# Causal attention with a two-layer cosine block: ScalarE's copies placed ahead of an exponential, and a new order in steps 0 and 1

## The chip, the cores and the metric

One core of a Trainium2 chip runs one program. The time is the device time of one execution in microseconds (us), from three runs. The engines named below are TensorE (PE), VectorE (DVE), ScalarE (ACT), GpSimd (POOL) and SyncE (SP), which issues most DMAs.

## The reference

Inputs: q, k and v of shape 4 x 12 x 448 x 64 (batch, heads, sequence, head dimension), `w_in` 768 x 2048 and `w_out` 2048 x 768, all float32. Causal attention is computed per head, the heads are laid side by side into x of 1792 x 768, and a two-layer block with h cos(h) between its products follows:

```python
scores = scale * np.matmul(q, k.transpose(0, 1, 3, 2))
scores = np.where(mask, -1000000000.0, scores)      # mask: above the diagonal
scores = scores - np.max(scores, axis=-1, keepdims=True)
attn = np.exp(scores)
attn = attn / (np.sum(attn, axis=-1, keepdims=True) + 1e-09)
x = np.matmul(attn, v)                              # then heads side by side
h = x @ w_in
out = (h * np.cos(h)) @ w_out
```

## The kernel before

The kernel has two stages that follow each other: `attention` (to about 160 us) and `moe` (the rest). The instructions of each engine run in the order in which the source issues them; the order below is written out by hand.

**Attention** works on 24 pairs of heads (4 batches x 6 pairs), `N = 24`, one a step. The loop at line 479 has 28 turns, because a pair passes through four steps: in step i-2 its q and k are loaded (`load_qk`), in step i-1 they are transposed (`transpose_in`, line 307, four transposes each) and copied from PSUM to SBUF (`evac_in`, line 319), in step i its probabilities are made, in step i+1 these are normalised and transposed (`tp`, line 400), and in step i+2 they are multiplied with v (`av`, line 421) and the output is split into a high and a low part (`finish_hi`, `finish_lo`).

A pair's 448 rows are cut into blocks m = 1 to 7 of 64 rows and 64 m columns; the two heads lie in the two halves of the 128 partitions, so block 7 is 128 x 448 and block 1 is 128 x 64. For a block, in order: `scores` (line 354, TensorE into PSUM banks 4 to 7), `masked` (line 363, VectorE: mask added, maximum taken, result to SBUF), `exps` (line 371, ScalarE: exponential and row sum, followed by a short read of the sum), `inverse` (lines 378 and 379, VectorE, for several blocks at once), `normalise` (line 385, GpSimd, in place). `FIRST` is blocks 7, 4, 3, which are normalised in their own step; `SECOND` is blocks 6, 1, 5, 2, which are normalised in the next step, after its first masking.

`tp` transposes 128 x 128 pieces of the probabilities in four groups (numbers 0 to 3) into PSUM banks; `evac_tp` copies a group to SBUF at line 315 (VectorE, groups 0 and 3) or 317 (ScalarE, groups 2 and 1). Group 1 is last and reuses bank 3, which group 0 left.

`finish_hi` (line 456, ScalarE) copies the output of `av` from PSUM rounded to fp32r, and `finish_lo` (line 460, VectorE) subtracts this from the output; `finish_lo` needs `finish_hi`.

In steps from 2 on, the orders of the engines are these. ScalarE: exponentials of 7, 4, 3, 6; `finish_hi`; copy of q for the next step; exponential of 1; copy of k; exponential of 5; copy of group 2; exponential of 2; copy of group 1. VectorE: masking of 7; inverse of `SECOND`; masking of 4, 3, 6, 1, 5, 2; inverse of `FIRST`; `finish_lo`; copies of groups 0 and 3; then, after the step's `yield`, half of the conversion of a weight piece (`convert_weight`, line 131: lines 139 and 142 in even steps, 148 and 152 in odd ones). GpSimd: normalising of 6, 1, 5, 2; what the conversion left to it (`postponed`, lines 145 or 156 and 157); normalising of 7, 4, 3. TensorE: scores; `av`; transposes of q; group 0; transposes of k; groups 3, 2, 1.

Before the loop, q and k of step 0 are copied in two halves by VectorE and ScalarE, and `keep_warm` issues matmuls on zeros that nothing reads.

**moe** multiplies x with the weights, which the attention stage and its own earlier groups have loaded and split into two fp32r parts.

Of the kernel before, what the change touches and what calls it, by code (L numbers as in the profile page):

```python
# [21 lines left out]
def kernel(  # L22
# [205 lines left out]
    def attention(filler_of, postponed):  # L228
        with (
# [53 lines left out]
            def keep_warm(n):  # L283
                for _ in range(n):
                    nc.tensor.matmul(
                        banks8[:, 0, 0:P], lhsT=warm, rhs=warm, start=True, stop=True
                    )
# [19 lines left out]
            def transpose_in(i, which, b):  # L307
                t = qkt[i, which] = flat[:, 2 * which + i % 2, 0:S], banks8[:, b, 0:S]
                o = t[1].rearrange("p (r c) -> p c r" if which else "p (c r) -> p c r", c=4)
                for c in range(4):  # L310
                    nc.tensor.transpose(o[:, c], nat[i][which][:, c], ident[0:Q4, 0:Q4])  # L311
# [7 lines left out]
            def evac_in(i, which, dve=False, rs=slice(0, Q4)):  # L319
                d, s = qkt[i, which]  # L320
                d = d.rearrange("p (r c) -> p r c", c=4)
                s = s.rearrange("p (r c) -> p r c" if which else "p (c r) -> p r c", c=4)
                evac(d[:, rs], s[:, rs], dve)
# [36 lines left out]
            def masked(i, *ms):  # L360
                for m in ms:
                    z = W if m == TURNED else S - m * R
                    nc.vector.tensor_tensor_reduce(  # L363
                        out=probs(i, m), in0=place(m), in1=mask[:, z : z + m * R], scale=-scale,
                        scalar=3.0e38, op0=ALU.add, op1=ALU.min, accum_out=stats[i][:, 0, col(m)],
                    )

            def exps(i, *ms):
                for m in ms:
                    st = stats[i]  # L370
                    nc.scalar.activation(  # L371
                        probs(i, m), probs(i, m), AF.Exp, scale=-1.0, bias=st[:, 0, col(m)],
                        accum_out=st[:, 1, col(m)],
                    )
# [3 lines left out]
                nc.vector.tensor_scalar(st[:, 2, cs], st[:, 1, cs], 1e-9, None, op0=ALU.add)  # L378
                nc.vector.reciprocal(st[:, 2, cs], st[:, 2, cs])  # L379

            def normalise(i, *ms):
                for m in ms:
                    p = probs(i, m)
                    r = stats[i][:, 2, col(m)]
                    nc.gpsimd.tensor_tensor(p, p, r.to_broadcast(list(p.shape)), op=ALU.mult)  # L385

# [11 lines left out]
            def tp(i, n, b, o=0):  # L400
                for x, (m, kc) in enumerate(ORDER[n]):
                    a = AT[m] + (m - 1 if kc == NM else 2 * kc + (m == TURNED))
                    nc.tensor.transpose(  # L403
                        banks8[:, b, o + x * P : o + (x + 1) * P],
                        prob[i][:, a * R : (a + 2) * R], ident,
                    )
# [14 lines left out]
            def av(i):  # L421
                (vn, vo), o = vals.pop(i), o_of(i).rearrange("p (n r) -> p n r", r=R)
                pt = ptr[i].rearrange("p n (s r) -> p n s r", r=R)
                for a in range(2):
                    s = spots[LAST[a][0], NM]
                    for y, m in enumerate(LAST[a]):
                        ys = slice(y * R, (y + 1) * R)
                        for j in range(2):
                            nc.tensor.matmul(
                                o[heads(j), ROW.index(m)],  # L430
                                lhsT=(vo[ys, a, i % 2] if y else vn[ys, m // 2])[:, heads(j)],
                                rhs=pt[ys, s, j ^ SWAP[m]],
                                start=a == 0, stop=False,
                            )
                runs = [((2, 4), 0), ((3, 5), 0), ((6,), 0), ((7,), 0), ((4, 5), 1), ((6, 7), 1), ((6, 7), 2)]
                for x, (ms, kc) in enumerate(runs):
                    s, z, n = spots[ms[0], kc], ROW.index(ms[0]), len(ms)
                    step = ms[-1] - ms[0] or 1
                    for j in range(2):
                        nc.tensor.matmul(  # L440
                            o[heads(j), z : z + step + 1 : step] if n == 2 else o[heads(j), z : z + 1],
                            lhsT=vn[:, kc, heads(j)], rhs=pt[:, s : s + n, j ^ SWAP[ms[0]]],
                            start=False, stop=x in (4, 6),
                        )
# [9 lines left out]
            def finish_hi(i):  # L454
                for hi, _, cs in x_of(i):
                    nc.scalar.copy(hi, o_of(i)[:, cs])

            def finish_lo(i):
                for hi, lo, cs in x_of(i):
                    nc.vector.tensor_tensor(lo, o_of(i)[:, cs], f32(hi), op=ALU.subtract)  # L460
# [3 lines left out]
            def fill(n):  # L464
                if not extra:
                    spare = itertools.cycle((7, 6))
                    extra.append(filler_of(lambda: banks8[:, next(spare)]))
                for _ in zip(range(n), extra[0]):
                    pass

            transpose_in(0, 1, 7)
            evac_in(0, 1, True, slice(0, Q4 // 2))
            evac_in(0, 1, False, slice(Q4 // 2, Q4))
            keep_warm(14)
            transpose_in(0, 0, QB)
            evac_in(0, 0, True, slice(0, Q4 // 2))
            evac_in(0, 0, False, slice(Q4 // 2, Q4))
            keep_warm(10)
            for i in range(N + 4):
                cur, prev, nxt = i < N, 0 < i <= N, i + 1 < N  # L480
                old = 0 <= i - 2 < N
                if i + 2 < N:
                    load_qk(i + 2)
                if prev:
                    load_v(i - 1)
                if cur:
                    open_step(i)
                    scores(i)
                    masked(i, 7)
                if prev:  # L490
                    inverse(i - 1, SECOND)
                    normalise(i - 1, *SECOND)
                while postponed:
                    postponed.pop(0)()
                if cur:
                    exps(i, 7)
                    masked(i, 4, 3)
                    if i == 0:
                        exps(i, 4)
                        transpose_in(i + 1, 0, QB)  # L500
                        evac_in(i + 1, 0, True)
                        transpose_in(i + 1, 1, 3)
                        evac_in(i + 1, 1)
                        keep_warm(8)
                        exps(i, 3)
                    else:
                        exps(i, 4, 3)
                    masked(i, 6, 1)
                    exps(i, 6)
                    masked(i, 5, 2)  # L510
                    inverse(i, FIRST)
                    normalise(i, *FIRST)
                if i == N + 2:
                    run(extra[0])
                if old:
                    av(i - 2)
                    finish_hi(i - 2)
                    finish_lo(i - 2)
                if nxt and i:
                    transpose_in(i + 1, 0, QB)  # L520
                    evac_in(i + 1, 0)
                if i == 1:
                    transpose_in(i + 1, 1, 1)
                    evac_in(i + 1, 1)
                if prev:
                    open_ptr(i - 1)
                    tp(i - 1, 0, 3)
                    evac_tp(i - 1, 0, 3, True)
                if N - 2 < i < N + 2:
                    fill((4, 12, 11)[i + 1 - N])  # L530
                if cur:
                    exps(i, 1)
                if nxt and i > 1:
                    transpose_in(i + 1, 1, 6)
                    evac_in(i + 1, 1)
                if cur:
                    exps(i, 5)
                if prev:
                    tp(i - 1, 3, 5)
                    evac_tp(i - 1, 3, 5, True)  # L540
                    tp(i - 1, 2, QB)
                    evac_tp(i - 1, 2, QB)
                if cur:
                    exps(i, 2)
                if prev:
                    tp(i - 1, 1, 3)
                    evac_tp(i - 1, 1, 3)
                yield i

    def m1_sum(ring, g, fi, t0, n, hv):  # L550
# [64 lines left out]
    def run(*gens):  # L615
        for x in gens:
            for _ in x:
                pass
# [777 lines left out]
```

## Time and profile before

| what | us |
|---|---|
| median of 3 runs (lowest, highest) | 615.96 (615.55, 619.16) |
| the profiled execution: its time | 615.92 |
| the profiled execution: span, first to last instruction | 613.9 |
| PE busy, share of the span | 599.3 (98%) |
| DVE busy | 474.6 (77%) |
| POOL busy | 451.8 (74%) |
| ACT busy | 409.2 (67%) |

Busy time counts the instructions on an engine; matmuls are pipelined and their ends are modelled, so a busy PE is not a PE at its peak. The mean granted TensorE clock was 0.999 of full speed. A row of a timeline gives the start, the duration, the engine, the line, the operation, what it wrote and read, and, in brackets, how long the engine had been idle before it and whose work ended that. Instructions of one kind in a row are merged into one row (x3).

### The profile page before, as it was taken

What the parts mean: (1) busy time and instruction counts of PE and PEld (TensorE: products, weight loads), DVE (VectorE), ACT (ScalarE), POOL (GpSimd) and SP (SyncE); (2) the same over time, 40 slices, a digit from 0 to 9 for tenths busy, and PEclk for the clock granted to TensorE, in tenths of its full rate; (3) what the DMA queues carried; (4) which work ended last, traced back from release to release, by engine and by line L of the source; (5) the groups of instructions that cost most, each with busy time, mean ns of one, the idle gap of its engine ahead of it and who ended that gap; (6) DMA issues with size and microseconds to landing.
All of it is one profiled execution on the core that took longest, in us unless ns stands there. A gap on an engine that the chain in (4) does not pass through costs nothing.

```text
span 613.9 us, 13441 instructions
## 1 busy us (share of the span) xinstructions
PE 599.3 (98%) x4788; PEld 546.6 (89%) x4788; DVE 474.6 (77%) x1017; ACT 409.2 (67%) x928; POOL 451.8 (74%) x529
## 2 busy tenths in 40 slices
PE   8999999999999999999999999999999999999996
PEld 7777787787788999999999999999999999999996
DVE  5899999999557788877778877754377887887786
ACT  5988888898677778787778777732435644653540
POOL 2767777687528879787777787753579888878994
PEclk9999999999999999999999999999999999999999
DMA  7656657558307859797796969489997559549104
GB/s 160 156 122 172 164 132 180 137 129 230 78 17 258 316 195 339 273 302 276 250 322 203 325 222 334 171 317 394 402 362 279 176 165 308 205 149 316 54 0 155
DMA packets 127010, 134.18 MB, mean 219 GB/s; under 512 B 75072, under 2 KB 111280, under 8 KB 126944
## 3 DMA queue, kind: packets, MB, share of 16 engines
q1 hardware_dynamic: 119264, 106.92, 55.6%
q0 software_dynamic: 4928, 24.78, 11.0%
q10 hardware_dynamic: 2752, 1.64, 0.9%
q8 instruction: 38, 0.62, 0.4%
q14 instruction: 28, 0.23, 0.1%
HBM read 83.36 MB, written 49.94 MB: 217 GB/s over the span
## 4 chain that ended last, share of the span: by engine, by line
PE 89%; DVE 6%; ACT 2%; POOL 1%; issue 1%; DVEq 0%; POOLq 0%; ACTq 0%
PE banks L652 22%; PE banks L1081 12%; PE banks L1101 12%; PE banks L557 7%; PE banks L558 7%; PE banks L556 7%; PE banks L354 5%; PE banks L440 5%; PE banks L403 3%; DVE pm L315 2%; PE banks L311 2%; PE banks L1118 2%; PE banks L1005 2%; DVE xa L460 2%; ACT pb L371 1%; DVE xb L460 1%
## 5 line engine op out<-in xcount | busy, mean ns | idle before, releaser
L640 DVE TENSOR_TENSOR acc<-acc,banks 128x768 f32<-128x768 f32 (+1 forms) x122 | 112.6, 932 | 43.6 <-PE banks L652 33.4
L385 POOL TENSOR_TENSOR pb<-pb,stat 128x448 f32<-128x448 f32 (+6 forms) x168 | 98.6, 617 | 45.5 <-DVE stat L379 43.3
L652 PE MATMUL banks<-w,gh 128*128 128x384 f32 x512 | 109.8, 335 | 0.0
L371 ACT ACTIVATE pb<-pb,stat 128x448 f32<-128x448 f32 (+6 forms) x168 | 84.9, 506 | 20.4 <-DVE stat L363 11.8
L652 PEld LDWEIGHTS banks<-w,gh 128*128 128x128 f32 x512 | 90.8, 188 | 1.5 <-DVE acc L638 0.2
L557 PE MATMUL banks<-xa,w 128*128 128x512 f32 x192 | 75.2, 391 | 0.0
L558 PE MATMUL banks<-xa,w 128*128 128x512 f32 x192 | 75.0, 391 | 0.0
L556 PE MATMUL banks<-xa,w 128*128 128x512 f32 x192 | 74.8, 390 | 0.0
L652 PE MATMUL banks<-w,gl 128*128 128x384 f32 x256 | 65.1, 335 | 0.0
L363 DVE CUSTOM_DVE_ANT_0 pb<-banks,mask 128x448 f32<-128x448 f32 (+6 forms) x168 | 61.2, 418 | 2.7 <-PE banks L354 2.7
L676 POOL TENSOR_TENSOR w<-ct,w 128x768 fp32r<-128x768 f32 x28 | 51.9, 1852 | 14.4 <-ACT w L675 9.1
L403 PE MATMUL banks<-ident,pb 128*128 128x128 f32 x336 | 52.9, 280 | 7.0 <-DVE pm L315 4.2
L564 ACT ACTIVATE ni<-banks 128x512 int32<-128x512 f32 (+1 forms) x64 | 34.4, 538 | 32.7 <-PE banks L558 19.2
L583 POOL TENSOR_TENSOR gl<-r,gh 128x512 fp32r<-128x512 f32 x32 | 41.5, 1298 | 19.5 <-ACT gh L582 19.2
L403 PEld LDWEIGHTS banks<-ident,pb 128*128 128x128 f32 x336 | 36.6, 141 | 17.0 <-DVE pm L315 9.5
L566 DVE SCALAR_TENSOR_TENSOR r<-ni,banks 128x512 f32<-128x512 int32 (+1 forms) x56 | 35.0, 626 | 21.4 <-ACT ni L564 20.7
L568 ACT ACTIVATE r<-r 128x512 f32<-128x512 f32 (+1 forms) x56 | 32.8, 586 | 22.4 <-DVE r L566 21.9
L652 PEld LDWEIGHTS banks<-w,gl 128*128 128x128 f32 x256 | 46.4, 188 | 0.0
L571 DVE SCALAR_TENSOR_TENSOR r<-r,banks 128x512 f32<-128x512 f32 (+1 forms) x56 | 35.0, 626 | 13.6 <-ACT r L569 13.6
L1081 PE MATMUL banks<-xb,bb 128*128 128x384 f32 x234 | 44.7, 334 | 0.0
L558 PEld LDWEIGHTS banks<-xa,w 128*128 128x128 f32 x192 | 36.0, 188 | 7.5
L1101 PE MATMUL banks<-big,gh 128*128 128x384 f32 x168 | 42.6, 334 | 0.0
(138 smaller groups left out, 1484.9 us busy)
## 6 DMA issues: line engine op xcount, KB each, us to landing
bb<-w_in_d SPq DMA_DIRECT2D x48, 384.0 KB, 5.2
land<-in_moe_w_in_dram SPq DMA_DIRECT2D x14, 768.0 KB, 6.0
land<-in_moe_w_out_dram SPq DMA_DIRECT2D x14, 768.0 KB, 5.6
w_out_d<-w POOLq DMA_DIRECT2D x14, 768.0 KB, 5.5
big<-w_out_d SPq DMA_DIRECT2D x25, 384.0 KB, 4.4
w_in_d<-w POOLq DMA_DIRECT2D x7, 768.0 KB, 4.3
raw_d<-ct POOLq DMA_DIRECT2D x14, 384.0 KB, 7.5
land<-in_k_dram SPq DMA_DIRECT2D x46, 112.0 KB, 3.2
```

The costliest lines, as they stand in the source:

```text
L363: nc.vector.tensor_tensor_reduce(out=probs(i, m), in0=place(m), in1=mask[:, z : z + m * R], scale=-scale, scalar=3.0e38, op0=ALU.add, op1= ...
L371: nc.scalar.activation(probs(i, m), probs(i, m), AF.Exp, scale=-1.0, bias=st[:, 0, col(m)], accum_out=st[:, 1, col(m)],)
L385: nc.gpsimd.tensor_tensor(p, p, r.to_broadcast(list(p.shape)), op=ALU.mult)
L403: nc.tensor.transpose(banks8[:, b, o + x * P : o + (x + 1) * P], prob[i][:, a * R : (a + 2) * R], ident,)
L556: yield nc.tensor.matmul(hv, lhsT=wh[:, f], rhs=x[:, 0, cc, t], start=(cc == 0), stop=False)
L557: yield nc.tensor.matmul(hv, lhsT=wh[:, f], rhs=x[:, 1, cc, t], start=False, stop=False)
L558: yield nc.tensor.matmul(hv, lhsT=wl[:, f], rhs=x[:, 0, cc, t], start=False, stop=(cc == NCC - 1))
L640: nc.vector.tensor_tensor(d, d, o, op=ALU.subtract)
L652: nc.tensor.matmul(o[:, e, 0:EH], lhsT=a[:, cs], rhs=w[:, e * EH : (e + 1) * EH], start=(x == 0), stop=(x == 5),)
L676: nc.gpsimd.tensor_tensor(w[:, 1], tf, f32(w[:, 0]), op=ALU.subtract)
L1081: nc.tensor.matmul(o, lhsT=w[:, u, k * P : (k + 1) * P], rhs=x[k][:, v], start=k + m == 0, stop=k == K - 1 and m == 2,)
L1101: nc.tensor.matmul(o[:, b % 2, 0:EH], lhsT=g_ops[i][u][:, c * P : (c + 1) * P], rhs=wouts[g, i][:, v], start=(x == 0), stop=(x == 2),)
```

## The change

`normalise` can be given an engine. In steps 2 to 23, ScalarE does `finish_hi` and the copy of q before the exponential of block 6, and the copy of k before that of block 1; the orders of the other engines are as they were. For step 0, q and k are copied whole, k by ScalarE and q by VectorE, with 8 warming matmuls behind instead of 10. Steps 0 and 1 get branches of their own: in step 0 the exponential of 3 comes ahead of the copy of k, and the inverse and normalising of `FIRST` ahead of the masking of 5 and 2. In step 1 VectorE makes the copies of q and k and normalises blocks 1 and 2 of step 0, the inverse of `SECOND` comes after the masking of 4 and 3, GpSimd normalises 6 and 5 alone, and group 1 goes to bank 0, ahead of groups 3 and 2.

```diff
-            def normalise(i, *ms):
+            def normalise(i, *ms, eng=nc.gpsimd):
                 for m in ms:
                     p = probs(i, m)
                     r = stats[i][:, 2, col(m)]
-                    nc.gpsimd.tensor_tensor(p, p, r.to_broadcast(list(p.shape)), op=ALU.mult)
+                    eng.tensor_tensor(p, p, r.to_broadcast(list(p.shape)), op=ALU.mult)
...
             transpose_in(0, 1, 7)
-            evac_in(0, 1, True, slice(0, Q4 // 2))
-            evac_in(0, 1, False, slice(Q4 // 2, Q4))
+            evac_in(0, 1)
             keep_warm(14)
             transpose_in(0, 0, QB)
-            evac_in(0, 0, True, slice(0, Q4 // 2))
-            evac_in(0, 0, False, slice(Q4 // 2, Q4))
-            keep_warm(10)
+            evac_in(0, 0, True)
+            keep_warm(8)
...
                     open_step(i)
                     scores(i)
                     masked(i, 7)
...
+                    exps(i, 7)
+                if i == 0:
+                    masked(i, 4, 3)
+                    exps(i, 4)
+                    transpose_in(i + 1, 0, QB)
+                    evac_in(i + 1, 0, True)
+                    transpose_in(i + 1, 1, 3)
+                    exps(i, 3)
+                    evac_in(i + 1, 1)
+                    keep_warm(8)
+                    masked(i, 6, 1)
+                    exps(i, 6, 1)
+                    inverse(i, FIRST)
+                    normalise(i, *FIRST)
+                    masked(i, 5, 2)
+                    exps(i, 5, 2)
+                elif i == 1:
+                    masked(i, 4, 3)
                     inverse(i - 1, SECOND)
+                    normalise(i - 1, 6, 5)
+                    normalise(i - 1, 1, 2, eng=nc.vector)
+                    exps(i, 4, 3)
+                    transpose_in(i + 1, 0, QB)
+                    evac_in(i + 1, 0, True)
+                    transpose_in(i + 1, 1, 1)
                     masked(i, 6, 1)
+                    evac_in(i + 1, 1, True)
+                    exps(i, 6, 1)
                     masked(i, 5, 2)
                     inverse(i, FIRST)
                     normalise(i, *FIRST)
                     open_ptr(i - 1)
                     tp(i - 1, 0, 3)
                     evac_tp(i - 1, 0, 3, True)
                     exps(i, 5)
+                    tp(i - 1, 1, 0)
                     tp(i - 1, 3, 5)
                     evac_tp(i - 1, 3, 5, True)
                     tp(i - 1, 2, QB)
+                    evac_tp(i - 1, 1, 0)
+                    exps(i, 2)
                     evac_tp(i - 1, 2, QB)
+                else:
...
+                    if cur:
+                        masked(i, 4, 3)
+                        exps(i, 4, 3)
+                        masked(i, 6, 1, 5, 2)
+                        inverse(i, FIRST)
+                        normalise(i, *FIRST)
+                    if i == N + 2:
+                        run(extra[0])
+                    if old:
+                        av(i - 2)
+                        finish_hi(i - 2)
+                        finish_lo(i - 2)
+                    if nxt:
+                        transpose_in(i + 1, 0, QB)
+                        evac_in(i + 1, 0)
+                    if cur:
+                        exps(i, 6)
+                    if prev:
+                        open_ptr(i - 1)
+                        tp(i - 1, 0, 3)
+                        evac_tp(i - 1, 0, 3, True)
+                    if N - 2 < i < N + 2:
+                        fill((4, 12, 11)[i + 1 - N])
+                    if nxt:
+                        transpose_in(i + 1, 1, 6)
+                        evac_in(i + 1, 1)
+                    if cur:
+                        exps(i, 1, 5)
...
```

## Rows read from the trace of the kernel before

**Rows 1.** Busy us (instructions) by engine, clock, DMA share, GB/s, in two stretches.
```profile
18.66:153.88 135.22, 131.16 (x2068) 106.54 (x2064) 124.58 (x490) 117.64 (x406) 102.03 (x177) 1.00 0.64 158
172.00:540.00 368.00, 368.00 (x1949) 345.65 (x1948) 271.88 (x359) 236.94 (x393) 276.68 (x263) 1.00 0.77 269
```

**Rows 2.** VectorE's groups, 18.66 to 153.88 us: busy, mean ns, idle before.
```profile
L460 DVE TENSOR_TENSOR xa<-banks,xa 128x448 fp32r<-128x448 f32 (+1 forms) x18 | 9.2, 514 | 6.4 <-ACT xa L456 4.2 <-ACT xb L456 2.2
...
L460 DVE TENSOR_TENSOR xb<-banks,xb 128x320 fp32r<-128x320 f32 (+1 forms) x9 | 4.8, 529 | 1.1 <-ACT xb L456 1.1
```

**Rows 3.** Timeline of step 5 (odd): start, duration, engine, line, operation.
```profile
38.46 0.67 ACT L371 ACTIVATE pb<-pb,stat 128x448 f32<-128x448 f32 x1 [0.88 <-DVE stat L363]
...
39.56 0.28 PE L440 MATMUL banks<-pm,vn 128*64 128x128 f32 x2
...
40.07 0.60 ACT L371 ACTIVATE pb<-pb,stat 128x384 f32<-128x384 f32 x1
...
40.67 0.51 ACT L456 CAST xa<-banks 128x448 fp32r<-128x448 f32 x1
40.73 0.17 DVE L379 RECIPROCAL stat<-stat 128x3 f32<-128x3 f32 x1
...
41.22 0.63 DVE L460 TENSOR_TENSOR xa<-banks,xa 128x448 fp32r<-128x448 f32 x1 [0.32 <-ACT xa L456]
...
42.49 0.20 PEld L403 LDWEIGHTS banks<-ident,pb 128*128 128x128 f32 x2 [0.41 <-DVE pm L315]
```

**Rows 4.** Timeline of GpSimd and VectorE at the end of step 5.
```profile
42.40 0.61 POOL L385 TENSOR_TENSOR pb<-pb,stat 128x256 f32<-128x256 f32 x1
...
42.95 0.80 DVE L148 SCALAR_TENSOR_TENSOR ct<-st,ct 128x256 uint32<-128x256 uint32 x1
...
42.97 0.51 POOL L385 TENSOR_TENSOR pb<-pb,stat 128x192 f32<-128x192 f32 x1
...
43.86 0.42 DVE L152 SCALAR_TENSOR_TENSOR ct<-st,ct 128x256 f32<-128x256 f32 x1
```

**Rows 5.** Timeline of VectorE and GpSimd in step 4 (even).
```profile
34.75 0.62 DVE L460 TENSOR_TENSOR xa<-banks,xa 128x448 fp32r<-128x448 f32 x1 [0.41 <-ACT xa L456]
...
35.57 0.94 POOL L385 TENSOR_TENSOR pb<-pb,stat 128x448 f32<-128x448 f32 x1
...
36.46 0.62 POOL L385 TENSOR_TENSOR pb<-pb,stat 128x256 f32<-128x256 f32 x1
...
36.48 0.75 DVE L139 TENSOR_SCALAR ct<-st 128x256 uint32<-128x256 uint32 x1
...
37.27 0.61 DVE L142 SCALAR_TENSOR_TENSOR ct<-st,ct 128x256 uint32<-128x256 uint32 x1
```

**Rows 6.** Timeline of GpSimd and VectorE at the end of step 18.
```profile
126.26 0.94 POOL L385 TENSOR_TENSOR pb<-pb,stat 128x448 f32<-128x448 f32 x1
...
127.00 0.35 DVE L139 TENSOR_SCALAR ct<-st 128x256 uint32<-128x256 uint32 x1
...
127.15 0.67 POOL L385 TENSOR_TENSOR pb<-pb,stat 128x256 f32<-128x256 f32 x1
...
127.39 0.72 DVE L142 SCALAR_TENSOR_TENSOR ct<-st,ct 128x256 uint32<-128x256 uint32 x1
```

**Rows 7.** Timeline of VectorE and ScalarE before and in step 0.
```profile
6.67 0.39 DVE L315 COPY flat<-banks 128x224 f32<-128x224 f32 x1 [0.78 <-PE banks L311]
...
7.09 0.34 ACT L317 COPY flat<-banks 128x224 f32<-128x224 f32 x1 [0.83 <-DVE flat L315]
...
9.88 0.62 DVE L315 COPY flat<-banks 128x448 f32<-128x448 f32 x1
```

**Rows 8.** Timeline of VectorE and GpSimd in step 1 and at its end.
```profile
13.20 0.52 DVE L378 TENSOR_SCALAR stat<-stat 128x4 f32<-128x4 f32 x1 [0.63 <-ACT pb L371]
...
14.12 0.82 POOL L385 TENSOR_TENSOR pb<-pb,stat 128x384 f32<-128x384 f32 x1
...
18.66 0.62 DVE L363 CUSTOM_DVE_ANT_0 pb<-banks,mask 128x448 f32<-128x448 f32 x1 [0.99 <-PE banks L354]
```

More of the change, by code (lines that the diff above doesn't have):

```diff
@@ L489, in attention @@
                     masked(i, 7)
-                if prev:
-                    inverse(i - 1, SECOND)
[L492 to L507, printed above, removed]
+                    exps(i, 7)
[16 more added lines that the diff above has]
+                    masked(i, 4, 3)
+                    inverse(i - 1, SECOND)
+                    normalise(i - 1, 6, 5)
[4 more added lines that the diff above has]
+                    transpose_in(i + 1, 1, 1)
                     masked(i, 6, 1)
-                    exps(i, 6)
+                    evac_in(i + 1, 1, True)
+                    exps(i, 6, 1)
                     masked(i, 5, 2)
@@ L512, in attention @@
                     normalise(i, *FIRST)
[L513 to L525, printed above, removed]
                     open_ptr(i - 1)
@@ L528, in attention @@
                     evac_tp(i - 1, 0, 3, True)
[L529 to L536, printed above, removed]
                     exps(i, 5)
-                if prev:
+                    tp(i - 1, 1, 0)
                     tp(i - 1, 3, 5)
@@ L541, in attention @@
                     tp(i - 1, 2, QB)
+                    evac_tp(i - 1, 1, 0)
+                    exps(i, 2)
                     evac_tp(i - 1, 2, QB)
[L543 to L547, printed above, removed]
+                else:
+                    if prev:
+                        inverse(i - 1, SECOND)
+                        normalise(i - 1, *SECOND)
+                    while postponed:
+                        postponed.pop(0)()
+                    if cur:
[15 more added lines that the diff above has]
+                        exps(i, 6)
+                    if prev:
+                        open_ptr(i - 1)
[8 more added lines that the diff above has]
+                        exps(i, 1, 5)
+                    if prev:
+                        tp(i - 1, 3, 5)
+                        evac_tp(i - 1, 3, 5, True)
+                        tp(i - 1, 2, QB)
+                        evac_tp(i - 1, 2, QB)
+                    if cur:
+                        exps(i, 2)
+                    if prev:
+                        tp(i - 1, 1, 3)
+                        evac_tp(i - 1, 1, 3)
                 yield i
```

## The prediction

> **What bounds the kernel now.** I read the busy time by stages first. From 172 to 540 us TensorE has no idle time at all, and from 18.66 to 153.88 us (attention steps 2 to 22, 135.22 us, so 6.44 us a step) it is TensorE 131.16 and VectorE 124.58 us [rows 1]. The second stage of the kernel is thus limited by TensorE and takes over where attention ends; what attention saves comes off the end one for one, and the question is only what a step of attention costs.
>
> Next, the groups of VectorE in that stage, for what ended its idle time: the low half of the output, `finish_lo`, waited 6.4 and 1.1 us for ScalarE's `finish_hi` [rows 2]. Of the stage's 10.6 us in which VectorE is not busy this one wait is 7.5, so nearly every step's VectorE work is a closed loop with one hole.
>
> Then one step in order of time [rows 3]. The last matmuls of `av` end at 39.56 + 0.28 = 39.84, so the output could be copied then. ScalarE takes the exponential of block 6 at 40.07 first and `finish_hi` at 40.67. VectorE has its last reciprocal done at 40.73 + 0.17 = 40.90 and begins `finish_lo` at 41.22, after 0.32 us of idle. Behind it on VectorE stand the two copies of transposed probabilities; the last transposes of the step wait 0.41 us for the first of these, and the next step's scores stand behind them on TensorE. After the copies VectorE converts a weight piece and opens the next step. Even and odd steps alternate: even ones wait 0.41 us [rows 5] and convert with lines 139 and 142, odd ones 0.32 us and lines 148 and 152.
>
> **Part 1: output and q ahead of the exponential of block 6 (steps 2 to 23).** `finish_hi` takes the slot of 40.07 and ends about 0.6 us earlier, at 40.58, before the reciprocal is done (40.90); since `av` ended 0.23 us before the slot, ScalarE does not wait. So `finish_lo` starts 0.32 us (odd) or 0.41 us (even) earlier. ScalarE's total is the same, and it idles 0.88 us before each step's first exponential [rows 3], which covers a shorter step; the exponential of block 2, for which the next inverse waits, keeps its place behind the same work. The order on TensorE, VectorE, GpSimd and of the loads on SP is unchanged in these steps, and no DMA is moved.
>
> What is late next is the conversion. Its operations meet GpSimd's normalising. In odd steps line 148 starts at 42.95 and lasts 0.80 us although line 152, the same size, takes 0.42; it ends 0.28 us after GpSimd's block 3 (42.97 + 0.51 = 43.48) [rows 4]. It waited for that instruction. GpSimd's instructions start when the previous step's inverse is ready, at the same distance from the step's start as before, so an earlier line 148 meets another of them. At 42.63 it falls into block 4 (42.40 to 43.01); let through at its end, it ends 0.28 later at 43.29 instead of 43.76. Line 152 then starts at 43.39 and ends at 43.81 if the way is free, or at 44.04 if it must wait for a block 3 pushed back by line 148's own 0.28, to 43.76; before it ended at 44.28. Gain 0.24 to 0.47; I take 0.38. In even steps line 139 comes at 36.48 - 0.41 = 36.07, inside block 7 (35.57 to 36.51), and line 142 then meets block 4 (36.46 to 37.08, a little later when pushed) instead of block 3 [rows 5].
>
> Whether GpSimd lets VectorE through between two of its instructions decides all of this, and one step of the trace shows it. In step 18 the conversion happened to come early: line 139 at 127.00 met block 7 (126.26 to 127.20) and ended at 127.35, 0.15 after it; line 142 at 127.39 met block 4 (127.15 to 127.82) and ended at 128.11, 0.29 after it, though block 3 was next on GpSimd [rows 6]. VectorE got in twice. By these two distances the even step's lines end at 36.66 and about 37.13 + 0.29 = 37.42, where they ended at 37.88: gain 0.45. The Trainium skill, in SBUF — State Buffer, section Who interferes with whom, says the shared port pair of VectorE and GpSimd is an exclusive lock; the trace agrees on the blocking, and who is next is taken up under the rivals.
>
> Sum over steps 3 to 22: nine even steps at 0.45, step 18 at 0.3 (it has part of the gain already), ten odd steps at 0.38: 8.15 us. Steps 2 and 23, at 0.32 each: 0.64.
>
> **Part 2: whole copies before step 0.** k is no longer halved and hides behind TensorE's warming matmuls. q: the first half starts on VectorE at 6.67, the second, on ScalarE, only after it, ending at 7.09 + 0.34 = 7.43. A whole copy of this size takes 0.62 us [rows 7], so 6.67 + 0.62 = 7.29: gain 0.14. Two fewer warming matmuls cost nothing: they only fill TensorE's wait for this copy. For the clock, the bounds are nothing and a dip over the few us of step 0; no row before 18.66 us shows one and TensorE's work is not spread thinner, so I take nothing.
>
> **Part 3: steps 0 and 1.** Here the order is new. VectorE gets the copies of q and k for step 2 (0.62 each) and the normalising of blocks 1 and 2; the inverse of the first blocks moves ahead of two maskings; the last transposes get bank 0 and no longer wait for a copy. In the trace VectorE idles 0.63 us before the inverse at 13.20 and 0.99 before step 2's first masking at 18.66, and that inverse's first operation took 0.52 us beside GpSimd [rows 8], where the reciprocal, as small, takes 0.17 [rows 3]; so there are some 1.97 us of room. Added are 1.24 us of copies and two normalisings of 64 and 128 columns, which no row shows on VectorE: each lies between nothing and line 152's 0.42 for 256 columns [rows 4], and I take 0.5 for both: 1.74. So +0.2 us of gain if nothing collides. The other bound is the second of VectorE's two normalisings waiting behind GpSimd's block 6 (0.82 us [rows 8]), released by the same reciprocal: a loss of 0.6. The upper bound is 0.5, if the earlier start of GpSimd's first normalising is also felt. Line 142, which waited when it followed line 139 directly [rows 6], is the nearest row, and it leans to the collision: I take a loss of 0.2. Exponential 3 ahead of the k copy delays step 1's scores by one exponential, less than the 0.60 us of block 6 [rows 3] and inside VectorE's idle 0.63.
>
> **Sum.** 8.15 + 0.64 + 0.14 - 0.2 = 8.7 us. The profiled execution took 615.92 us (span 613.9 and 2.0 around it), 0.04 under the median of 615.96. Forecast: 615.92 - 8.7 = **607.2 us**. Its own range, with odd steps at 0.24 to 0.47 and part 3 from -0.6 to +0.5: 605.6 to 609.0.
>
> **Rivals.**
> A, GpSimd keeps the pair. At each boundary its next instruction, already queued, starts ahead of the waiting VectorE. Then lines 148 and 142 end where they end now, behind block 3, and the earlier `finish_lo` buys nothing: steady gain 0. In step 1 both of VectorE's normalisings wait, for block 6 (0.82) and for the smaller block 5 (at most as long again): 0.2 - 1.6 = -1.4, plus 0.14. Time 615.92 + 1.3 = 617.2, slower than before. It decides if VectorE, arriving well inside one GpSimd instruction, is passed by the next. For it: lines 148 and 139, arriving within 0.05 us of a boundary, were passed [rows 4, 5]. Against it: step 18. The same section of the Trainium skill says that whoever starts first holds the lock for its whole instruction; GpSimd's successor starts 0.05 us before its predecessor ends [rows 5], which by that wording would favour this rival. Chance 0.12.
>
> B, half the gain. Either VectorE gets through in even steps only (nine at 0.45, step 18 and the other parts: 4.9 us, 611.0), or `finish_hi`, now first in ScalarE's queue, waits for `av` once the step is shorter: its slack is 0.23 us, and the exponentials of 6, 1, 5 and 2 stand behind it. A `finish_hi` late by 0.2 us cuts each step's gain about in half, again near 611. Against it: `av` follows the same copies on VectorE and moves with them. Chance 0.18.
>
> C, more than forecast. TensorE's own waits in a step are 0.41 us and a shorter one for the q copy, which now also goes; if conversion and normalising never meet, steps could save 0.55: near 604. Chance 0.07.
>
> **Chances.** Forecast 0.60, A 0.12, B 0.18, C 0.07, and 0.03 for a loss that no row shows. A change of under 1% (6.2 us) is about what a measurement cannot tell from none. Faster by over 1%: forecast and C, 0.67, and 0.02 from the better end of B: 0.69. Within 1%: A and the rest of B, 0.28. Slower: 0.03. The range that leaves out two in ten reaches from the better part of C through most of B: 604.8 to 611.5.
>
> **What would show it.** Right: VectorE's wait for `finish_hi` gone from its groups; a step of 6.0 to 6.05 us; lines 139 and 148 ending 0.15 and 0.28 us after a GpSimd block 7 or 4, no longer after block 3; step 2 opening 0.1 to 0.6 us around 18.66. Wrong: line 148 still ending behind block 3 at an unchanged 6.4 us (A); ScalarE idle before `finish_hi` (B); step 2 opening past 19.5.

## The result, and the profile after

The changed kernel takes **608.41 us** (median of 6 runs, 607.76 to 610.53), the kernel before, run beside it, 616.23 (6 runs, 615.55 to 619.16): a ratio of 0.987, 95% interval 0.985 to 0.990. The forecast was 607.2, with a range of 604.8 to 611.5. The profiled execution took 608.03 us (span 606.2), 7.89 less than the one before; the forecast sum was 8.7.

The busy time of the same two stretches comes first: us, then busy us (instructions) of PE, PEld, DVE, ACT and POOL, clock, DMA share and GB/s. The first stretch again opens with step 2's first masking and ends with step 23's.

```profile
18.54:146.27 127.73, 127.56 (x2066) 107.11 (x2068) 124.72 (x490) 118.20 (x406) 106.19 (x179) 1.00 0.67 166
172.00:540.00 368.00, 368.00 (x1961) 347.11 (x1960) 274.65 (x365) 236.51 (x395) 278.60 (x264) 1.00 0.78 271
```

Attention steps 2 to 22 take 127.73 us where they took 135.22 [rows 1]: 6.08 a step instead of 6.44. The second stage is still TensorE from end to end. In the first TensorE's row is now busy too for 127.56 us of 127.73, but it isn't the limit there yet: with the same matmuls a step still gets shorter in an experiment below (5.83 us). VectorE now idles 3.0 us of the stretch instead of 10.6, and its groups say which hole closed (busy us, mean ns, idle before):

```profile
L460 DVE TENSOR_TENSOR xa<-banks,xa 128x448 fp32r<-128x448 f32 (+1 forms) x18 | 8.7, 484 | 0.0
L142 DVE SCALAR_TENSOR_TENSOR ct<-st,ct 128x256 uint32<-128x256 uint32 x11 | 7.8, 709 | 0.4
L148 DVE SCALAR_TENSOR_TENSOR ct<-st,ct 128x256 uint32<-128x256 uint32 x10 | 7.1, 715 | 0.0
L139 DVE TENSOR_SCALAR ct<-st 128x256 uint32<-128x256 uint32 x11 | 6.9, 629 | 0.0
L152 DVE SCALAR_TENSOR_TENSOR ct<-st,ct 128x256 f32<-128x256 f32 x10 | 5.4, 541 | 1.0
L460 DVE TENSOR_TENSOR xb<-banks,xb 128x320 fp32r<-128x320 f32 (+1 forms) x9 | 4.7, 519 | 0.0
```

`finish_lo` waits for nothing; before it waited 7.5 us [rows 2]. VectorE's busy time is the same as before (124.72 us, before 124.58), however: the conversion's lines still take 541 to 715 ns on average. What they take when no GpSimd instruction runs is measured below.

Step 5 (odd, opening at 37.08) in order of time, ScalarE and VectorE:

```profile
37.74 0.67 ACT L371 ACTIVATE pb<-pb,stat 128x448 f32<-128x448 f32 x1 [0.17 <-DVE stat L363]
...
39.35 0.51 ACT L456 CAST xa<-banks 128x448 fp32r<-128x448 f32 x1
...
40.01 0.17 DVE L379 RECIPROCAL stat<-stat 128x3 f32<-128x3 f32 x1
40.10 0.59 DVE L460 TENSOR_TENSOR xa<-banks,xa 128x448 fp32r<-128x448 f32 x1
...
40.26 0.62 ACT L371 ACTIVATE pb<-pb,stat 128x384 f32<-128x384 f32 x1
```

`finish_hi` ends at 39.86, before the reciprocal (40.18), and `finish_lo` follows that reciprocal at once (in the record its start even overlaps the reciprocal's end by 0.08 us). ScalarE's idle time before the step's first exponential has gone from 0.88 us [rows 3] to 0.17: it covered the shorter step, and there is little left.

Now the conversion and GpSimd, in step 5:

```profile
41.67 0.61 POOL L385 TENSOR_TENSOR pb<-pb,stat 128x256 f32<-128x256 f32 x1
41.81 0.76 DVE L148 SCALAR_TENSOR_TENSOR ct<-st,ct 128x256 uint32<-128x256 uint32 x1
42.25 0.69 POOL L385 TENSOR_TENSOR pb<-pb,stat 128x192 f32<-128x192 f32 x1
42.68 0.54 DVE L152 SCALAR_TENSOR_TENSOR ct<-st,ct 128x256 f32<-128x256 f32 x1
```

and in step 6 (even, opening at 43.14):

```profile
47.42 0.94 POOL L385 TENSOR_TENSOR pb<-pb,stat 128x448 f32<-128x448 f32 x1
47.81 0.69 DVE L139 TENSOR_SCALAR ct<-st 128x256 uint32<-128x256 uint32 x1
48.31 0.67 POOL L385 TENSOR_TENSOR pb<-pb,stat 128x256 f32<-128x256 f32 x1
48.54 0.72 DVE L142 SCALAR_TENSOR_TENSOR ct<-st,ct 128x256 uint32<-128x256 uint32 x1
48.94 0.69 POOL L385 TENSOR_TENSOR pb<-pb,stat 128x192 f32<-128x192 f32 x1
```

Line 148 ends at 42.57, 0.29 after block 4 (42.28), although block 3 was next on GpSimd; line 139 ends 0.14 after block 7, line 142 0.28 after block 4. Each time VectorE got in between two GpSimd instructions that follow each other without a gap, and the one that it passed got longer: block 3 takes 0.69 where it took 0.51 [rows 4]. Line 152 then waits for this stretched block 3 (to 42.94) and ends 0.28 after it.

### The profile page after: what moved, and what is told of

Read it like the earlier page. It is cut to its first block, busy times and chain, and to the rows that moved or that the text cites. A ratio compares the mean times of both kernels' runs of the same rounds, so it can differ in the third digit from the quotient of the medians.

```text
span 606.2 us, 13434 instructions
## 1 busy us (share of the span) xinstructions
PE 595.4 (98%) x4786; PEld 546.6 (90%) x4786; DVE 475.7 (78%) x1020; ACT 409.0 (67%) x925; POOL 455.1 (75%) x527
## 4 chain that ended last, share of the span: by engine, by line
PE 75%; DVE 21%; issue 2%; DMA 1%; POOL 0%; ACTq 0%; ACT 0%; DVEq 0%; POOLq 0%
PE banks L678 22%; PE banks L1107 13%; PE banks L1127 13%; DVE pb L363 9%; PE banks L583 7%; PE banks L584 7%; PE banks L582 7%; DVE pm L315 4%; PE banks L1144 2%; PE banks L1031 2%; DVE ct L148 1%; DVE xa L460 1%; DVE stat L379 1%; DVE ct L152 1%; DVE ct L139 1%
## 5 line engine op out<-in xcount | busy, mean ns | idle before, releaser
L385 POOL TENSOR_TENSOR pb<-pb,stat 128x448 f32<-128x448 f32 (+6 forms) x166 | 101.9, 643 | 34.3 <-DVE stat L379 32.4
L403 PE MATMUL banks<-ident,pb 128*128 128x128 f32 x336 | 48.0, 277 | 1.6 <-POOL pb L385 0.9
L354 PE MATMUL banks<-flat 64*64 64x64 f32 (+5 forms) x768 | 42.6, 356 | 1.2 <-DVE stat L379 0.7
L354 PEld LDWEIGHTS banks<-flat 64*64 64x64 f32 x768 | 30.8, 133 | 13.6 <-issue 2.5
```

The source lines that it names most:

```text
L354: nc.tensor.matmul(place(m)[heads(j ^ SWAP[m]), c : c + z - a], lhsT=qt[heads(j), (m - 1) * R : m * R], rhs=kt[heads(j), a:z], start=banks ...
L385: eng.tensor_tensor(p, p, r.to_broadcast(list(p.shape)), op=ALU.mult)
```

## The experiments

Every ratio is to the kernel before, run beside the kernels on the same chip.

### Part 1 alone

The kernel before, with nothing but the new order on ScalarE in steps from 2 on:

```diff
                     masked(i, 6, 1)
-                    exps(i, 6)
+                    if i < 2:
+                        exps(i, 6)
...
                     evac_in(i + 1, 0)
+                if cur and i > 1:
+                    exps(i, 6)
...
-                if cur:
+                if cur and i < 2:
                     exps(i, 1)
...
                     evac_in(i + 1, 1)
+                if cur and i > 1:
+                    exps(i, 1)
```

> The kernel before with part 1 alone: from step 2 on ScalarE does the output and q ahead of block 6 and k ahead of block 1; the start and steps 0 and 1 are as before. Theory (the gain is part 1, and the new steps 0 and 1 lose what the whole copies win): step 2 opens at 18.66 us as before, lasts about 5.9, then steps of 6.05; ratio to before 0.986, about 607.8 us, a little under the changed kernel. Rival (the new steps 0 and 1 carry a share of the gain): 610 us or more, ratio 0.990 and up.

608.40 us (4 runs, 607.34 to 609.55), ratio 0.986 (0.983 to 0.989). Step 2 opens at 18.65 as before, takes 5.83 us, and the steps behind it 6.05 to 6.08 (step 18 6.35). The whole gain is in part 1; the ratio can't be told from the changed kernel's (0.985 to 0.990).

### Steps 0 and 1 alone

The changed kernel with the old order on ScalarE in steps from 2 on:

```diff
-                        masked(i, 6, 1, 5, 2)
+                        masked(i, 6, 1)
+                        exps(i, 6)
+                        masked(i, 5, 2)
...
                         evac_in(i + 1, 0)
-                    if cur:
-                        exps(i, 6)
...
+                    if cur:
+                        exps(i, 1)
                     if nxt:
                         transpose_in(i + 1, 1, 6)
                         evac_in(i + 1, 1)
                     if cur:
-                        exps(i, 1, 5)
+                        exps(i, 5)
```

> The changed kernel with ScalarE's old order from step 2 on; whole copies and the new steps 0 and 1 stay. Theory: VectorE waits for the high half again, steps of 6.4 to 6.5 us as before; step 2 opens near 18.5 and is longer than before because VectorE's inverse meets GpSimd's late normalising: ratio 1.000, within 0.002. Rival (steps 0 and 1 carry a share): 0.996 or less.

616.44 us (10 runs), ratio 0.9986 (0.9970 to 1.0001). The hole in VectorE is back:

```profile
L460 DVE TENSOR_TENSOR xa<-banks,xa 128x448 fp32r<-128x448 f32 (+1 forms) x18 | 9.2, 514 | 6.1 <-ACT xa L456 3.9 <-ACT xb L456 2.2
```

Without part 1 the other two parts change the time by no more than 0.3%.

### Which of the two copies matters

First only the output ahead of the exponential of block 6, the q copy behind it; then the reverse, the q copy ahead and the output behind. The edits to the changed kernel:

```diff
                         finish_lo(i - 2)
+                    if cur:
+                        exps(i, 6)
                     if nxt:
                         transpose_in(i + 1, 0, QB)
                         evac_in(i + 1, 0)
-                    if cur:
-                        exps(i, 6)
```

```diff
                         av(i - 2)
-                        finish_hi(i - 2)
-                        finish_lo(i - 2)
                     if nxt:
...
                     if cur:
                         exps(i, 6)
+                    if old:
+                        finish_hi(i - 2)
+                        finish_lo(i - 2)
```

> The changed kernel with the copy of q put back behind the exponential of block 6; the output's high half alone stays ahead of it. Theory (only the output's wait on VectorE was the price; q is needed by TensorE later and has slack): steps of 6.05 us, ratio 0.987 as the changed kernel, within 0.002. Rival (q ahead also pays, since TensorE waited for it before its third group of transposes): steps of 6.15 to 6.25, ratio 0.991 to 0.994.

> The changed kernel with the output's high half put behind the copy of q and the exponential of block 6, later than in the kernel before: the wait of VectorE made longer. Theory (a step is the loop reciprocal, wait, low half, copy, transposes, scores, masking): the high half starts near 3.65 us after the step's first masking instead of 2.9, the low half at 4.2 instead of 3.4, steps of 6.9 us or a little more; 21 steps by 0.45 us: about 625 us, ratio 1.015. Rival (the conversion and GpSimd set the step, the wait is hidden in them): steps of 6.4 to 6.5, ratio 1.00.

The first takes 608.92 us (4 runs, 607.88 to 609.12; ratio 0.983 to 0.989), with steps of 6.04 to 6.06 from 4 on (step 18 6.35): where the q copy stands makes no difference that these runs can show. The second takes 635.47 (ratio 1.027 to 1.032), with steps of mostly 7.20 and 7.42. One odd step of it:

```profile
43.54 0.53 ACT L317 COPY flat<-banks 128x448 f32<-128x448 f32 x1 [0.56 <-PE banks L311]
43.97 0.62 ACT L371 ACTIVATE pb<-pb,stat 128x384 f32<-128x384 f32 x1
...
44.57 0.52 ACT L456 CAST xa<-banks 128x448 fp32r<-128x448 f32 x1
...
45.13 0.62 DVE L460 TENSOR_TENSOR xa<-banks,xa 128x448 fp32r<-128x448 f32 x1 [1.42 <-ACT xa L456]
```

The direction was right and the size too small (about 625 us was expected): ScalarE first waits for q's transposes, and `finish_hi` stands behind that wait as well as behind the copy and the exponential. `finish_lo` starts 4.53 us into a step of 7.20, thus 2.67 before the next step opens. In step 5 of before the two lay 2.98 apart (41.22 [rows 3]; step 6 opened at 44.20). The step does hang on `finish_lo`; how far behind it the next one opens depends on what the conversion meets.

### No GpSimd instruction beside the conversion

From step 2 on, blocks 7, 4 and 3 are not normalised at all:

```diff
-                        normalise(i, *FIRST)      # steps from 2 on
```

> The changed kernel with the normalising of blocks 7, 4 and 3 left out from step 2 on, so that GpSimd is idle while VectorE converts; those probabilities stay unnormalised. Theory (what now sets a step is VectorE, and its conversion waits for GpSimd): lines 139, 142, 148 and 152 last 0.28, 0.43, about 0.45 and 0.43 us instead of 0.69, 0.72, 0.77 and 0.54; a step falls from 6.05 to the next limit, low half plus 2.67 us, 5.7 to 5.85: 4 to 7 us less than the changed kernel, 601.5 to 604.5. Rival (TensorE or ScalarE already sets 6.05): steps stay at 6.0 or more, 607 or more.

604.43 us (2 runs, 604.08 and 604.77), ratio 0.981 (0.977 to 0.984). Steps from 4 on take 5.83 us:

```profile
54.35 0.41 DVE L148 SCALAR_TENSOR_TENSOR ct<-st,ct 128x256 uint32<-128x256 uint32 x1
54.87 0.42 DVE L152 SCALAR_TENSOR_TENSOR ct<-st,ct 128x256 f32<-128x256 f32 x1
55.31 0.62 DVE L363 CUSTOM_DVE_ANT_0 pb<-banks,mask 128x448 f32<-128x448 f32 x1
60.18 0.28 DVE L139 TENSOR_SCALAR ct<-st 128x256 uint32<-128x256 uint32 x1
60.50 0.42 DVE L142 SCALAR_TENSOR_TENSOR ct<-st,ct 128x256 uint32<-128x256 uint32 x1
61.15 0.62 DVE L363 CUSTOM_DVE_ANT_0 pb<-banks,mask 128x448 f32<-128x448 f32 x1 [0.22 <-PE banks L354]
```

Free of GpSimd, the four lines take 0.28, 0.42, 0.41 and 0.42 us; what they take above that in the changed kernel is waiting. TensorE loses almost no wait by this edit: in the changed kernel its transposes waited for a normalised block once in the stretch, 0.3 us. With VectorE's waiting gone a step falls from 6.04 or 6.06 to 5.83. At the end of an even step the next masking now waits 0.22 us for TensorE's scores; at the end of an odd one it follows the conversion at once (55.29, 55.31), so there VectorE still sets the step.

### The conversion's rounding moved on GpSimd

Can that 0.2 us be had without leaving work out? In even steps lines 156 and 157 (the rounding that the conversion leaves to GpSimd) go behind the normalising of 7, 4 and 3, so that this comes earlier. One kernel has this edit alone, another also the edit of the next experiment.

```diff
-                    while postponed:
+                    while postponed and (i % 2 or not cur):
                         postponed.pop(0)()
...
                         normalise(i, *FIRST)
+                    while postponed:
+                        postponed.pop(0)()
```

> The changed kernel with GpSimd's part of an even step's conversion (lines 156 and 157, 1.1 us) moved behind its normalising of 7, 4 and 3, which then starts at about 3.2 us of the step instead of 4.3. Theory: line 139, coming at 4.74, meets block 3 (4.7 to 5.2) and ends near 5.35, line 142 meets line 156 (0.4) and ends near 5.85: even steps 5.8 instead of 6.04, odd ones unchanged; ten by 0.24: about 606, ratio 0.983. Rival (another limit at 6.0, or line 139 passed at the boundary near 4.7): even steps of 6.0 or more, ratio 0.987.

> The edits of e6 and e8 together, as a kernel that might beat both. Theory: they add up, about 605 us, ratio 0.981 to 0.982. Rival: no better than the changed kernel, 0.987.

611.51 us (608.86 to 611.89) and 610.00 (609.73 to 610.24), where 606 and 605 were expected: no gain, but a loss. Steps 3 to 22 of the first take 124.27 us together, in the changed kernel 121.30. Even steps became shorter (5.72 us in many, near the 5.8 expected), but many odd ones longer (6.33), and step 22 took 10.22 us in the first kernel and 9.84 in the second. The trace has a reason for each. In step 21, which opens at 133.69:

```profile
133.91 0.73 POOL L157 TENSOR_TENSOR w<-ct,w 128x256 fp32r<-128x256 f32 x1
134.24 0.42 DVE L378 TENSOR_SCALAR stat<-stat 128x4 f32<-128x4 f32 x1
```

The first operation of the odd step's inverse, 0.16 to 0.17 us where it meets nothing, meets the late line 157 and takes 0.42; GpSimd's second group and then its first come later with it. And SyncE's longest wait, from 120 to 142 us (us, times, longest):

```profile
SPq L204 <- POOL w L156: 5.4, 1, 5.4
```

The store of the rounded weights, at line 204, waits 5.4 us for the late rounding, and the loads of v for step 22 stand behind it in SyncE's order. In the changed kernel the same store waits 3.0 us, and the first of these loads is issued 4.7 us before step 22 opens (135.52, 140.23); here it is 2.3 us (137.71, 140.01):

```profile
133.85 0.34 SPq L204 DMA_DIRECT2D w_out_d<-w  x1
...
137.71 1.96 SPq L265 DMA_DIRECT2D vn<-in_v_dram  x2
```

In step 22 TensorE's `av` then waits for v, `finish_hi` for `av`, and `finish_lo` 3.99 us for `finish_hi`:

```profile
147.05 0.62 DVE L460 TENSOR_TENSOR xb<-banks,xb 128x448 fp32r<-128x448 f32 x1 [3.99 <-ACT xb L456]
```

An instruction moved on GpSimd thus reached the end of the chain over a store that the expectation had left out.

### Step 1 without VectorE's two normalisings

```diff
-                    normalise(i - 1, 6, 5)
-                    normalise(i - 1, 1, 2, eng=nc.vector)
+                    normalise(i - 1, *SECOND)
```

> The changed kernel with all four blocks of the second group normalised by GpSimd in step 1 again, as before the change. Theory (in step 1 VectorE's two normalisings took 1.08 us because the second waited for GpSimd's block 6, and everything behind them on VectorE, the inverse for GpSimd's next group too, came late and cost step 2 as well): VectorE's first 1.0 us of loss goes, step 2 opens 0.3 to 0.7 us earlier and lasts 5.85 to 6.1 instead of 6.43: 0.8 to 1.2 us less than the changed kernel, about 607.4. Rival (GpSimd, with two blocks more, is late for TensorE's transposes and gives it all back): no gain, 608.4.

607.72 us (606.91 to 608.02). It was run again beside the changed kernel on one chip, with two kernels that single out part 2: this one with the old halved copies in front of step 0, and the kernel before with whole copies and nothing else.

```diff
-            evac_in(0, 1, True, slice(0, Q4 // 2))     # kernel before, whole copies only
-            evac_in(0, 1, False, slice(Q4 // 2, Q4))
+            evac_in(0, 1)
...
-            evac_in(0, 0, True, slice(0, Q4 // 2))
-            evac_in(0, 0, False, slice(Q4 // 2, Q4))
-            keep_warm(10)
+            evac_in(0, 0, True)
+            keep_warm(8)
```

> The changed kernel once more, beside the next on the same chip: 608.4, step 1 at 6.35 and step 2 at 6.43 again, VectorE's second normalising in step 1 waiting for GpSimd's block 6.

> The changed kernel with all of SECOND normalised by GpSimd in step 1, once more. If the collision in step 1 costs what the traces say (steps 1 and 2 together 11.85 instead of 12.78), it is 0.6 to 1.0 us faster than the changed kernel on the same chip: 607.6. If that difference was only the start of its runs: the same as the changed kernel, 608.4.

> The changed kernel with all of SECOND normalised by GpSimd in step 1 and, in addition, the halved copies of before in front of step 0. Theory: as the kernel with the normalising on GpSimd alone, 607.7, within 0.3; step 0's first masking 1.85 us after the first half's start. Rival (whole copies matter): 0.3 to 0.6 us slower than that kernel on the same chip.

> The kernel before with part 2 alone: k and q of step 0 copied whole, 8 warming matmuls behind q. Theory: from the start of the q copy to step 0's first masking 1.79 us where the halves took 1.85 (6.67 to 8.52), a gain of 0.06 and not the 0.14 of the prediction, lost in what q's landing varies from run to run; the steps from 2 on as before (6.40 / 6.51); time 616, ratio 1.000. Rival (the prediction's size, or more: the copies are worth what the longer start of other runs hides): 0.14 us or more, step 0 opening at 8.38 or earlier beside a q that lands as before.

| kernel | us (lowest, highest), runs | start of q copy to step 3 |
|---|---|---|
| before | 616.46 (615.53, 618.53), 17 | 18.19 |
| before, whole copies only | 616.51 (615.63, 618.17), 12 | 18.07 |
| before, part 1 only (another chip; before there 617.11) | 608.40 (607.34, 609.55), 4 | 17.82 |
| changed | 608.81 (608.68, 610.34), 5 | 18.42 |
| changed, GpSimd alone in step 1 | 607.75 (607.17, 608.11), 4 | 17.49 |
| the same, halved copies | 607.83 (607.37, 608.18), 4 | 17.81 |

The last column is from the profiled executions: from VectorE's (first) copy of q before step 0 to the first masking of step 3. So it leaves out when that copy starts, which is told below. The changed kernel without VectorE's normalisings is 1.06 us faster than the changed kernel, and their runs don't overlap; by the column it is 0.93. It is the best version found: 0.985 of before (0.9835 to 0.987). Whole copies alone don't change the time (ratio 1.0003, 0.9989 to 1.0016) and save 0.12 us in the column. With the halves back in the best version the column is 0.32 longer, 0.06 of it at the copy and 0.25 in step 2 (6.09 for 5.84), but the medians differ by 0.08 only; why step 2 differs was not settled, and so nothing firm is said for or against part 2.

What happens in step 1 of the changed kernel, VectorE and GpSimd:

```profile
13.77 1.08 DVE L385 TENSOR_TENSOR pb<-pb,stat 128x64 f32<-128x64 f32 x2
13.88 0.83 POOL L385 TENSOR_TENSOR pb<-pb,stat 128x384 f32<-128x384 f32 x1 [0.59 <-DVE stat L379]
...
15.89 0.62 ACT L371 ACTIVATE pb<-pb,stat 128x384 f32<-128x384 f32 x1 [1.33 <-DVE stat L363]
...
17.08 0.15 DVE L378 TENSOR_SCALAR stat<-stat 128x3 f32<-128x3 f32 x1
...
17.59 1.97 POOL L385 TENSOR_TENSOR pb<-pb,stat 128x448 f32<-128x448 f32 x3 [2.16 <-DVE stat L379]
...
19.08 0.51 DVE L378 TENSOR_SCALAR stat<-stat 128x4 f32<-128x4 f32 x1
```

VectorE's pair takes 1.08 us, its second waiting for GpSimd's block 6 (13.88 to 14.71). The masking of 6 comes late, ScalarE idles 1.33 us, the inverse of the first blocks comes only at 17.08, and GpSimd's first group, from 17.59 to 19.56, reaches into step 2, whose inverse at 19.08 takes 0.51 us for it. With GpSimd alone, in a step that opens 0.08 later, the same inverse and group are a us earlier:

```profile
16.01 0.17 DVE L378 TENSOR_SCALAR stat<-stat 128x3 f32<-128x3 f32 x1
...
16.54 1.97 POOL L385 TENSOR_TENSOR pb<-pb,stat 128x448 f32<-128x448 f32 x3 [0.46 <-DVE stat L379]
```

## Why the prediction was right, and which sizes were off

**Part 1, the even steps: right.** Nine steps at 0.45 were forecast; they went from 6.51 to 6.04, so 0.47. Line 139 ends behind block 7 and line 142 behind block 4, at the distances read from step 18 [rows 6].

**The odd steps: right, a little high.** 0.38 was taken between 0.24 and 0.47; measured 0.34 (6.40 to 6.06). Line 148 ends 5.49 us after the opening, where the working put it. Line 152 took the worse branch, behind the block 3 that line 148 had pushed back; that block ends 0.18 later than before relative to the opening (5.86 against 5.68), not 0.28.

**Step 18: 0.03 in place of 0.3, and read wrongly.** The prediction said that the conversion "happened to come early" there. Line 139 began 5.31 us into that step, in most even steps 5.20; block 7 ended at 5.52, elsewhere at 5.22. So it was GpSimd that came late. Its first instruction in step 18 of the changed kernel, and the inverse that meets a later one:

```profile
117.09 0.83 POOL L385 TENSOR_TENSOR pb<-pb,stat 128x384 f32<-128x384 f32 x1 [1.55 <-DVE stat L363]
...
118.12 0.72 POOL L385 TENSOR_TENSOR pb<-pb,stat 128x320 f32<-128x320 f32 x1
118.42 0.46 DVE L378 TENSOR_SCALAR stat<-stat 128x3 f32<-128x3 f32 x1
```

In the other even steps that idle time is 1.26 us. In before it was 2.09 against 1.79. The kernels with part 1 alone, steps 0 and 1 alone and whole copies alone have the same 0.3; the changed kernel with GpSimd alone in step 1, and the one without the normalising of 7, 4 and 3, don't. What causes it stays open. In the changed kernel it costs 0.29 us; the best version doesn't have it (step 18 takes 6.05).

**Steps 3 to 22 together:** 129.02 to 121.30, 7.72 us of the 8.15 forecast.

**Part 2: 0.06 at the copy, forecast 0.14.** From the start of the copy to step 0's first masking it is 1.79 us instead of 1.85. The whole copy is done 0.62 us after its start, the halves 0.76, as the prediction had it; but TensorE's first scores follow VectorE's whole copy by 0.15 us (7.16, 7.31) and ScalarE's half by 0.06 (7.43, 7.49), which the prediction left out. Before and after:

```profile
7.49 1.74 PE L354 MATMUL banks<-flat 64*64 64x64 f32 x32 [0.30 <-ACT flat L317]
7.31 1.74 PE L354 MATMUL banks<-flat 64*64 64x64 f32 x32 [0.36 <-DVE flat L315]
```

By the column, which goes on to step 3, it is 0.12. Either is less than the start varies from run to run.

**Part 3 with step 2: the term that failed.** A gain of 0.32 in step 2, 0.14 from the copies and a loss of 0.2 in steps 0 and 1 make 0.26; the column above lost 0.24 (18.19 to 18.43 in the first profile of the changed kernel). By the kernel with part 1 alone, step 2 was worth 0.37 (forecast 0.32); the copies give 0.12; so the new order of steps 0 and 1 cost about 0.7, just past its lower bound of 0.6. The collision of VectorE's second normalising with GpSimd's block 6 was named, and its price was within the bounds: the pair took 1.08 us, between the 0.5 of the free case and the 1.3 of the bound. What was missed is what stood behind: the inverse of the first blocks, 4.89 us into the step (17.08) where it had been 3.74, and GpSimd's group that reached into step 2 for it. The question that was asked in part 1, where GpSimd's next group will lie, was not asked in part 3.

**Step 23 and the end: about 0.2, forecast 0.32.** From step 23's opening to the end of the span it was 460.1 us and is 459.9; in the kernels with whole copies alone and part 1 alone it was 460.4 and 460.2, and over all kernels here it goes from 459.7 to 460.4. The spread is larger than the term, so what the last step saves can't be told.

**The sum: near, and in part by luck.** In the profiled executions the span is 7.78 us shorter: 7.72 in steps 3 to 22, less 0.24 before them, about 0.17 at the end, and 0.13 because VectorE's copy of q began at 6.54 us and not at 6.67, which is chance: two profiles of the changed kernel have 6.54 and 7.17 (see the last section). The mechanism of part 1 is right; what the forecast of 8.7 lacked is part 3, about 0.5 us more than its 0.2 of loss, and 0.4 in the steps.

**The rivals.** A (GpSimd keeps the pair) is refuted: in every step from 3 on, line 148 or 142 ends 0.28 us behind block 4, although block 3 follows that without a gap. In SBUF — State Buffer, section Who interferes with whom, the Trainium skill says that whoever issues first gets the shared pair for the whole instruction. The rows above agree: the VectorE instruction, which had been waiting for 0.44 to 0.55 us, began before GpSimd's successor (41.81 and 42.25) and went ahead of it. The prediction had counted the successor's early start for A. Within 0.05 us of a boundary the record doesn't tell who will be first: line 148 of before began 0.02 us ahead of block 3 and was passed [rows 4], while in step 2 of the changed kernel line 139 began 0.01 us ahead of block 3 and waited for nothing:

```profile
23.92 0.29 DVE L139 TENSOR_SCALAR ct<-st 128x256 uint32<-128x256 uint32 x1
23.93 0.64 POOL L385 TENSOR_TENSOR pb<-pb,stat 128x192 f32<-128x192 f32 x1
```

B's second form, `finish_hi` waiting for `av`, shows only in step 2 (0.16 us). C was had only by leaving the normalising out: 604.4, which is the price that C gave.

## What to carry to other kernels

A wait between two engines is worth its length only until the next resource on the same engine; work out, for the instruction that comes earlier, which instruction of the other engine it will now meet, and where that one's end has moved. A step that differs from its neighbours is the best evidence in a trace, but ask first which of its two engines is off its usual place. When work is put on a second engine to balance it, follow the first engine's next group all the way into the next step; and when an instruction is moved behind others, look on every queue, the one that issues stores and loads too, for what waits for it.

## What the runs showed of the hardware that was not expected

Some VectorE instructions that read and write SBUF alone wait for a running GpSimd `TENSOR_TENSOR`, whatever their size: those of lines 139, 142, 148, 152 and 378, and the normalising at 385. The 128x4 one at line 378 took 0.51 us instead of 0.16. Not all do: the reciprocal at line 379 takes 0.17 to 0.18 us in every step, with GpSimd running beside it or not. The copies and maskings from PSUM, `finish_lo` too, show no such stretch beside GpSimd. The waiting shows as busy time, not as idle time, so no view of waits lists it; the mean durations of one line in two kernels do.

After such a wait less is left than the free time. Line 139 ends 0.15 us behind GpSimd's instruction (0.28 free), lines 142, 148 and 152 end 0.28 behind it (0.41 to 0.42 free), and line 378 ends 0.03 behind it (19.59 and 19.56 above; 0.16 free). So in each about 0.13 to 0.15 us lie beside GpSimd's record, and one that begins that close to GpSimd's end shows no stretch, as line 378 in most steps.

The start varies more than part 2 is worth. VectorE's copy of q, which waits for TensorE's transposes of q, began between 6.46 and 7.17 us in the profiles of the last four kernels (6.67 in that of before), and everything after moved with it. The time from there to the first masking was 1.85 us with halves and 1.79 with the whole copy, every time. In three of the four the transposes began within 0.14 us of q's landing (5.71, 5.94 and 6.14). In the changed kernel's second profile q landed at 6.03 and they began at 6.58, behind warming matmuls that took longer than in its first profile. First profile, then second:

```profile
4.68 0.95 PE L285 MATMUL banks<-warm 128*128 128x128 bf16 x14
5.40 1.34 PE L285 MATMUL banks<-warm 128*128 128x128 bf16 x14
6.58 0.55 PE L311 MATMUL banks<-ident,land 112*128 112x112 f32 x4
```

The traces record the full granted clock (2.4 GHz) from 3.88 us on in the first and only from 6.22 in the second; before that a warming matmul began every 0.107 us, behind it every 0.056.
